# Retention attention with two expert layers: another order of the first twelve attention visits' matmuls, and first weights converted in fixed visits

## The chip, the cores and the metric

One core of a Trainium2 chip runs the kernel. The metric is the device time of one execution in microseconds. Six queues work side by side on a core: TensorE (PE) multiplies, VectorE (DVE), ScalarE (ACT) and GpSimd (POOL) do elementwise work, SyncE (SP) issues most of the DMAs, and each engine works through its own instructions in the order in which they were written, waiting for the others by semaphores.

## The reference

```python
def _attn_ref(q, k, v):                       # (4, 8, 576, 64) each
    scores = scale * np.matmul(q, k.transpose(0, 1, 3, 2))
    gamma = 1.0 - 2.0 ** (-5.0 - np.arange(H))
    Dmat = np.where(rel >= 0, gamma[:, None, None] ** rel[None, :, :], 0.0)
    return np.matmul(scores * Dmat, v)

def _moe_ref(x, w1, w2, w3, w_out):           # x: (2304, 512), d_ff 768
    h = np.maximum(np.maximum(x @ w1, x @ w2), x @ w3)
    return h @ w_out

def _moe2_ref(x, w_gate, w_val, w_out):       # d_ff 1536
    g = x @ w_gate
    return (g * (1.0 / (1.0 + np.exp(-g))) * (x @ w_val)) @ w_out
```

The attention's output, heads side by side, is the first layer's x, and that layer's output is the second's.

## The kernel before

Attention is done in **units**: one of four batches, a pair of heads and one half (288 positions) of the sequence, 32 units in all, in the order batch, pair, half. A half is three chunks of 96 positions. For a unit PE makes: the transposes of k (`tp`, line 249) and those of q with its decay (line 252), both in `a_prep`; the scores of each chunk (`s`, `a_score`, line 272); the chunk's sums of weighted k times v (`m_ps`, `a_state`, line 288), from which ACT and DVE build the running state `st`; and in `a_value` (line 311) the output `o_ps`, which has **v products** (masked scores `pT` times v) and **state products** (`st` times q, six matmuls in a second half and four in a first). The weighted k, `ks`, is a POOL instruction (line 242) at the head of `a_prep`. DVE multiplies the scores by the mask (`pT`, line 274); ACT and DVE split the output into a high and a low part, `xh` and `xl`. A matmul uses the PE array in a shape, rows by columns: transposes of k 96\*128, those of q, v products and m_ps 96\*64, state products 64\*64, scores 64\*96, the dense layers 128\*128. From unit 12 on, the transposes are made by DVE instead.

The first layer's weights come as 64-bit floats. `conv_steps` turns one 128 x 512 piece (a **weight** below, 18 in all) into a high half `wh` and a low half `wlo`, in six phases: two ACT copies `wz` and `wl`, two DVE steps on `wz` (lines 130, 131), one DVE step `wl` (line 133), ACT `wh` (line 141) and POOL `wlo` (line 143). A **slice** (`f_slice`, line 440) is 12 matmuls of one weight with the `xh` and `xl` of one batch half; its result is copied by ACT for the first of three matrices and joined to `hmax` by DVE for the others (line 446). Slices use two rotating PSUM banks (`ps_mm`), a visit's `o_ps` one bank of its own.

The order is written out by hand: a loop of 16 **visits**, one unit each, and then pairs of units. `visit(n)` makes unit n's output, then scores and states of unit n + 1, and in between the preparation of unit n + 2 (`a_prep`), slices and conversion phases. Visits 0 to 7 have no slices; visits 8 to 15 have 4, 4, 4, 4, 4, 4, 6 and 6. `sharing` makes a list of phases from the number of conversions of the visit and spreads it over the gaps between its slices (`share(j)`, ahead of slice j or behind the last one).

Of the kernel before, what the change touches and what calls it, by code (L numbers as in the profile page):

```python
# [10 lines left out]
F32 = mybir.dt.float32  # L11
# [12 lines left out]
P = 128  # L24
NP = H // 2
CK = 96
NC = 3
C = CK * NC
# [41 lines left out]
def retention_moe(ctx, tc, consts, q, k, v, w1, w2, w3, w_out, w_gate, w_val, w_out2, out):  # L70
    nc = tc.nc
    pe, act, dve, pool, sp = nc.tensor, nc.scalar, nc.vector, nc.gpsimd, nc.sync
# [77 lines left out]
    PT = 12  # L150
    PP = 16
# [110 lines left out]
    def a_score(n):  # L262
        if n >= NU:
            return
        b, h, pr = units[n]
        u = U[n]
        s = psa.tile([CK, 2, 512], F32, name="s", tag="s")
        for c in range(NC):
            cs = slice(c * CK, (c + 1) * CK)
            for e in range(2):  # L270
                hd = slice(64 * e, 64 * e + 64)
                pe.matmul(s[:, e, cs], u["kt"][hd, cs], u["qg"][hd, c], start=True, stop=True)  # L272
        pT = att.tile([CK, 2, NC, CK], F32, name="pT", tag="pT")
        dve.tensor_tensor(pT, s[:, :, 0:C].rearrange("p e (c m) -> p e c m", c=NC),
                          d_t[pr].unsqueeze(2).to_broadcast([CK, 2, NC, CK]), ALU.mult)
        u["pT"] = pT

    def a_state(n):

        if n >= NU:  # L280
            return
        b, h, pr = units[n]
        u = U[n]
        nk = NC - h
        m = psa.tile([P, NC, D], F32, name="m_ps", tag="m_ps")
        for c in range(nk):
            for e in range(2):
                pe.matmul(m[64 * e:64 * e + 64, c], u["ks"][:, c, e], u["v"][:, c, e], start=True, stop=True)  # L288
        if h == 0:
            st = states[(b, pr)] = att.tile([P, 2 * NC, D], F32, name="st", tag="st", bufs=2)  # L290
        else:
            st = states.pop((b, pr))
        for c in range(nk):
            g = h * NC + c
            if g == 0:
                act.activation(st[:, 1], m[:, c], ACTF.Copy)
            else:
                dve.scalar_tensor_tensor(st[:, g + 1], st[:, g], e_t[:, pr:pr + 1], m[:, c], ALU.mult, ALU.add)
        u["st"] = st

    def a_value(n):
        b, h, pr = units[n]
        u = U.pop(n)
        o = psa.tile([P, C], F32, name="o_ps", tag="o_ps")
        inter = [(c, e, u["st"][64 * e:64 * e + 64, h * NC + c], u["qg"][64 * e:64 * e + 64, c])
                 for c in range(1 - h, NC) for e in range(2)]
        intra = [(c, e, u["v"][:, c, e], u["pT"][:, e, c]) for c in range(NC) for e in range(2)]
        seen = set()
        parts = intra + inter if n <= NQ0 else inter + intra
        for i, (c, e, l, r) in enumerate(parts):  # L310
            pe.matmul(o[64 * e:64 * e + 64, c * CK:(c + 1) * CK], l, r, start=e not in seen,  # L311
                      stop=(c, e) not in [x[:2] for x in parts[i + 1:]], skip_group_check=True)
            seen.add(e)
        xh, xl = [ffn.tile([P, C], F32R, name=f"x{x}", tag=f"x{x}{pr}", bufs=4) for x in "hl"]
        act.activation(xh, o, ACTF.Copy)
        xs[(2 * b + h, pr)] = (xh, xl)
        return lambda: dve.tensor_tensor(xl, o, f(xh), ALU.subtract)
# [93 lines left out]
    def conv_plan(convs):  # L411

        for _ in range(convs):
            i = wc[0]
            if i < len(win_units):
                wc[0] += 1
                yield (i, 2), (i + 1, 0)
                yield (i, 3), (i + 1, 1)
                yield (i, 4), (i, 5)
# [41 lines left out]
            ps = ps_mm.tile([P, 512], F32, name="psz", tag="mm")  # L461
            pe.matmul(ps.rearrange("p (a m) -> p a m", m=P), zero, zero.unsqueeze(1).to_broadcast([P, 4, P]), start=True, stop=True)

    def sharing(spread, convs, joins):
        plan = list(conv_plan(convs))
        done = 0

        def share(j):
            nonlocal done
            upto = len(plan) * (j + 1) // (spread + 1)  # L470
            for step in plan[done:upto]:
                for i, ph in step:
                    win_phase(i, ph)
            done = upto
            if joins:
                for _ in range(1 if j % 2 else 2):
                    next(early, None)

        return share

    def visit(n, slices, convs):
        share = sharing(slices, convs, False)
        low = a_value(n)
        if slices:
            share(0)
        if n % 2:
            a_load(n // 2 + 3)
        if n % 2 == 0:
            t_load(n // 2 + 2)
        elif n == PP - 1:  # L490
            t_load(PP // 2 + 2)
        if n % (2 * NP) == 2 * NP - 1:
            fq.extend((n // NP - 1 + h, *w) for w in win_units for h in range(2))
        if n < NQ0:
            a_score(n + 1)
            low()
            a_state(n + 1)
            late = []
        elif n + 1 < PP:
            a_state(n + 1)  # L500
            low()
            a_score(n + 1)
            late = []
        else:
            low()
            swap_banks()
            late = pair_next(PP // 2)
        ahead = [n + 2] if n < PP - 2 else [PP, PP + 1] if n < PP - 1 else [PP + 2, PP + 3]
        for j in range(slices + 1):
            if late:  # L510
                late.pop(0)()
            if j == min(2, slices - 1) or not slices:
                a_prep(ahead.pop(0))
            if j == 4 and ahead:
                a_prep(ahead.pop(0))
            if j or not slices:
                share(j)
            if j < slices:
                f_some(1)
# [82 lines left out]
    def tables(pr):  # L602
        g = 2 * NC
        (pool if pr else dve).tensor_tensor(
            dia[pr].rearrange("p a e m -> p (a e) m"), ident.unsqueeze(1).to_broadcast([CK, g, CK]),
            q_t[:, g * pr:g * pr + g].unsqueeze(2).to_broadcast([CK, g, CK]), ALU.mult)
        pool.tensor_tensor(d_t[pr], mask.unsqueeze(1).to_broadcast([CK, 2, CK]),
                           s_t[:, 2 * pr:2 * pr + 2].unsqueeze(2).to_broadcast([CK, 2, CK]), ALU.mult)
# [7 lines left out]
    a_prep(0)  # L616
    spin(2)
    a_score(0)
    a_prep(1)
    a_state(0)  # L620
    for n in range(PP):
        if n < NP - 1:
            tables(n + 1)
        if 2 <= n < 6:
            win_load(n - 2)
        if n == 5:
            win_phase(0, 0)
            win_phase(0, 1)
        if n == 9:
            sp.dma_start(out=cst_g, in_=consts[:, O_G:NCONST])  # L630
        visit(n, *((0, 0) if n < 5 else (0, 1) if n < 8 else (4, 2) if n < 13 else (4, 3) if n < 14 else (6, 2)))
        if n == 15:
            ask(1)
    for j in range(PP // 2, NU // 2):
# [442 lines left out]
```

## Time and profile before

| | us |
|---|---|
| runs | 818.52, 820.24, 821.1 |
| median of the three | 820.24 |
| the profiled execution | 818.73 |
| its span, first to last instruction | 816.9 |
| PE busy in it | 808.5 (99%) |
| DVE busy | 563.2 (69%) |
| ACT busy | 315.1 (39%) |
| POOL busy | 211.1 (26%) |

The granted TensorE clock is at its full level in all of the span's forty slices. A row of the order of time gives the start and the length of an instruction or of a run of like ones, and in brackets how long the engine had been idle and what ended that. Matmuls overlap, so the length of a piece is best read from one row's start to the next row's start.

### The profile page before, as it was taken

To read this page: it belongs to the slowest core of one execution; us is meant where nothing else is said; L and a number is where in the kernel's file an instruction comes from. 1 tells how busy PE (TensorE), PEld (TensorE's weight loads), DVE (VectorE), ACT (ScalarE), POOL (GpSimd) and SP (SyncE) were. 2 spreads that over 40 slices of the span, in tenths; PEclk is the share of its full clock that TensorE was granted. 3 is DMA by queue.
4 is the path that set the end of the run, shared out by engine and by line. 5 is a ranking of instruction groups with operands and counts; after the bars stand their busy time and mean duration, and the time that the engine had idled before them with its cause. 6 is when DMAs were issued, how large, how long until landed. Compare 5 with 4: busy or idle time off the path is not lost.

```text
span 816.9 us, 15439 instructions
## 1 busy us (share of the span) xinstructions
PE 808.5 (99%) x5924; PEld 759.6 (93%) x5924; DVE 563.2 (69%) x1008; ACT 315.1 (39%) x633; POOL 211.1 (26%) x193
## 2 busy tenths in 40 slices
PE   9999999999999999999999999999999999999998
PEld 6799899999999999999999999999999999999996
DVE  3768857777774245586387889998888865455555
ACT  3654514324322133664345534444444322332220
POOL 5344320000000003342032223332332233322331
PEclk9999999999999999999999999999999999999999
DMA  9999779999963143964534343444322016666522
GB/s 193 243 227 206 167 148 238 260 249 240 252 184 113 64 137 106 285 159 149 190 116 157 127 149 141 149 168 153 132 77 71 20 65 243 208 232 219 200 97 77
DMA packets 158201, 135.08 MB, mean 165 GB/s; under 512 B 94000, under 2 KB 132912, under 8 KB 158128
## 3 DMA queue, kind: packets, MB, share of 16 engines
q1 hardware_dynamic: 157568, 133.69, 57.4%
q8 instruction: 46, 0.75, 0.4%
q10 hardware_dynamic: 560, 0.42, 0.2%
q14 instruction: 27, 0.22, 0.1%
HBM read 89.77 MB, written 44.30 MB: 164 GB/s over the span
## 4 chain that ended last, share of the span: by engine, by line
PE 93%; DVE 4%; ACT 1%; issue 1%; DMA 0%; POOL 0%; SPq 0%; ACTq 0%; DVEq 0%
PE g L945 31%; PE ps L440 28%; PE ps L922 18%; PE ps L869 7%; PE o_ps L311 2%; PE s L272 1%; PE o_ps L332 1%; PE s L362 1%; PE o_ps L327 1%; PE tp L252 1%; PE m_ps L288 1%; PE s L355 0%; DMA kn<-in_k_dram 0%; PE tp L249 0%; DVE acc L927 0%
## 5 line engine op out<-in xcount | busy, mean ns | idle before, releaser
L440 PE MATMUL ps<-xl,wh 128*128 128x288 f32 x576 | 172.2, 299 | 1.8 <-DVE hmax L446 1.2
L440 PE MATMUL ps<-xh,wh 128*128 128x288 f32 x576 | 169.8, 295 | 0.0
L440 PE MATMUL ps<-xh,wlo 128*128 128x288 f32 x576 | 169.6, 294 | 0.0
L993 POOL TENSOR_TENSOR gl<-p,gh 128x384 fp32r<-128x384 f32 x72 | 86.0, 1212 | 287.3 <-ACT gh L992 277.5
L922 PE MATMUL ps<-wp,gh 128*128 128x512 f32 (+1 forms) x436 | 135.6, 392 | 0.4 <-DVE acc L927 0.3
L440 PEld LDWEIGHTS ps<-xl,wh 128*128 128x128 f32 x576 | 108.0, 188 | 5.2 <-DVE hmax L446 2.4
L440 PEld LDWEIGHTS ps<-xh,wlo 128*128 128x128 f32 x576 | 108.1, 188 | 0.0
L440 PEld LDWEIGHTS ps<-xh,wh 128*128 128x128 f32 x576 | 108.1, 188 | 0.0
L922 PEld LDWEIGHTS ps<-wp,gh 128*128 128x128 f32 x436 | 80.5, 188 | 15.0 <-DVE acc L927 1.5
L922 PE MATMUL ps<-wp,gl 128*128 128x512 f32 (+1 forms) x218 | 85.6, 393 | 0.0
L446 DVE TENSOR_TENSOR hmax<-ps,hmax 128x288 f32<-128x288 f32 x96 | 43.5, 454 | 58.1 <-PE ps L440 49.1
L927 DVE TENSOR_TENSOR acc<-ps,acc 128x512 f32<-128x512 f32 (+1 forms) x91 | 61.8, 682 | 27.8 <-PE ps L922 26.6
L945 PE MATMUL g<-xhB,wa 128*128 128x384 f32 x288 | 73.3, 336 | 0.0
L945 PE MATMUL g<-xhT,wc 128*128 128x384 f32 x288 | 73.2, 335 | 0.0
L672 POOL TENSOR_TENSOR hl<-hf,hh 128x384 fp32r<-128x384 f32 x26 | 30.6, 1186 | 133.7 <-ACT hh L671 131.5
L992 ACT ACTIVATE gh<-p 128x384 fp32r<-128x384 f32 x72 | 37.9, 526 | 58.6 <-DVE p L996 51.6
L981 ACT ACTIVATE sb<-u 128x384 f32<-128x384 f32 x36 | 18.9, 525 | 100.3 <-DVE u L979 99.2
L242 POOL TENSOR_TENSOR ks<-kn,cst_a 96x384 f32<-96x384 f32 (+1 forms) x32 | 24.6, 779 | 115.5 <-PE s L355 105.4
L444 ACT ACTIVATE hmax<-ps 128x288 f32<-128x288 f32 x48 | 19.7, 410 | 84.5 <-PE ps L440 83.3
L945 PEld LDWEIGHTS g<-xhB,wa 128*128 128x128 f32 x288 | 52.1, 188 | 0.0
L945 PEld LDWEIGHTS g<-xhT,wc 128*128 128x128 f32 x288 | 52.0, 188 | 0.0
L973 DVE TENSOR_TENSOR p<-g,p 128x384 f32<-128x384 f32 x36 | 19.9, 554 | 43.8 <-PE g L945 34.7
(134 smaller groups left out, 1699.1 us busy)
## 6 DMA issues: line engine op xcount, KB each, us to landing
w<-in_moe_w_out_dram SPq DMA_DIRECT2D x18, 512.0 KB, 4.1
w<-l_d SPq DMA_DIRECT2D x28, 256.0 KB, 3.0
h_d<-hmax SPq DMA_DIRECT2D x48, 144.0 KB, 3.1
w<-in_moe_w_dram SPq DMA_DIRECT2D x12, 512.0 KB, 7.1
w<-in_moe_w_gate_dram SPq DMA_DIRECT2D x12, 512.0 KB, 5.3
w<-in_moe_w_val_dram SPq DMA_DIRECT2D x12, 512.0 KB, 5.5
vn<-in_v_dram SPq DMA_DIRECT2D x16, 288.0 KB, 7.6
out_dram<-acc SPq DMA_DIRECT2D x17, 256.0 KB, 2.0
```

What stands on the lines that cost most here:

```text
L242: pool.tensor_tensor(u["ks"][:, 0:nk], u["k"][:, 0:nk], sc, ALU.mult)
L440: pe.matmul(ps, l[:, ksl], r, start=n == 0, stop=n == 3 * KD - 1)
L444: act.activation(mx[hb], ps, ACTF.Copy)
L446: dve.tensor_tensor(mx[hb], ps, mx[hb], ALU.max)
L672: (dve if fi in (3, 5) and hx else pool).tensor_tensor(hl, hf, f(hh), ALU.subtract)
L869: pe.matmul(ps[:, 0:HT], l[:, es], rr, start=n == 0, stop=n == 3 * F1 - 1)
L922: pe.matmul(ps[:, cs], l[:, sl], r[:, cs], start=n == 0, stop=n == 3 * GRP - 1)
L927: dve.tensor_tensor(a[:, cs], ps[:, cs], a[:, cs], ALU.add)
L945: pe.matmul(ps, l[:, ks], r[:, kc], start=first and n == 0, stop=n == 5, skip_group_check=True)
L973: dve.tensor_tensor(p5, g2, p5, ALU.add)
L992: act.activation(gh[half], t, ACTF.Copy)
L993: pool.tensor_tensor(gl[half], t, f(gh[half]), ALU.subtract)
```

## The change

Visits 0 to 7 get a function of their own, `visit_first`, and `a_value` takes a hook `between`. A visit now prepares unit n + 1 first (`a_prep(n + 1)`, up to unit 11), then does unit n's v products, the hook (the states of unit n + 1), unit n's state products, and the scores of unit n + 1. Visit 7 does the states behind the scores, as before. In visits 0 to 7 the output is put into the slices' two banks (`o_mm`). The low part `xl` of a visit is made in the next one. Tables `FIRST` and `NEXT` name the phases of the first weights in visits 4 to 8, one weight and a half fewer than before by the end of visit 7; the count of conversions starts again at weight 4 with visit 9. Visits 8 to 15 now have 4, 4, 4, 4, 4, 5, 6 and 5 slices, and conversions of 2, 3, 2, 2, 3 and 2 weights in visits 9 to 14.

```diff
@@ -298,19 +298,23 @@
                 dve.scalar_tensor_tensor(st[:, g + 1], st[:, g], e_t[:, pr:pr + 1], m[:, c], ALU.mult, ALU.add)
         u["st"] = st
 
-    def a_value(n):
+    def a_value(n, between=lambda: None):
         b, h, pr = units[n]
         u = U.pop(n)
-        o = psa.tile([P, C], F32, name="o_ps", tag="o_ps")
-        inter = [(c, e, u["st"][64 * e:64 * e + 64, h * NC + c], u["qg"][64 * e:64 * e + 64, c])
-                 for c in range(1 - h, NC) for e in range(2)]
-        intra = [(c, e, u["v"][:, c, e], u["pT"][:, e, c]) for c in range(NC) for e in range(2)]
-        seen = set()
-        parts = intra + inter if n <= NQ0 else inter + intra
-        for i, (c, e, l, r) in enumerate(parts):
-            pe.matmul(o[64 * e:64 * e + 64, c * CK:(c + 1) * CK], l, r, start=e not in seen,
-                      stop=(c, e) not in [x[:2] for x in parts[i + 1:]], skip_group_check=True)
-            seen.add(e)
+        if n < NQ0:
+            o = ps_mm.tile([P, 512], F32, name="o_mm", tag="mm")[:, 0:C]
+        else:
+            o = psa.tile([P, C], F32, name="o_ps", tag="o_ps")
+        for c in range(NC):
+            for e in range(2):
+                pe.matmul(o[64 * e:64 * e + 64, c * CK:(c + 1) * CK], u["v"][:, c, e], u["pT"][:, e, c],
+                          start=c == 0, stop=c < 1 - h, skip_group_check=True)
+        between()
+        for c in range(1 - h, NC):
+            for e in range(2):
+                hd = slice(64 * e, 64 * e + 64)
+                pe.matmul(o[hd, c * CK:(c + 1) * CK], u["st"][hd, h * NC + c], u["qg"][hd, c],
+                          start=False, stop=True, skip_group_check=True)
         xh, xl = [ffn.tile([P, C], F32R, name=f"x{x}", tag=f"x{x}{pr}", bufs=4) for x in "hl"]
         act.activation(xh, o, ACTF.Copy)
         xs[(2 * b + h, pr)] = (xh, xl)
@@ -461,8 +465,8 @@
             ps = ps_mm.tile([P, 512], F32, name="psz", tag="mm")
             pe.matmul(ps.rearrange("p (a m) -> p a m", m=P), zero, zero.unsqueeze(1).to_broadcast([P, 4, P]), start=True, stop=True)
 
-    def sharing(spread, convs, joins):
-        plan = list(conv_plan(convs))
+    def sharing(spread, convs, joins, plan=None):
+        plan = plan or list(conv_plan(convs))
         done = 0
 
         def share(j):
@@ -478,11 +482,45 @@
 
         return share
 
+    FIRST = {4: ((0, 0), (0, 1)), 5: ((0, 2),), 6: ((0, 3), (1, 0), (0, 4), (0, 5)), 7: ((1, 1), (1, 2))}
+    NEXT = [((1, 3), (2, 0), (1, 4), (1, 5)), ((2, 1),), ((2, 2), (3, 0)), ((2, 3), (3, 1)), ((2, 4), (2, 5)),
+            ((3, 2),), ((3, 3), (4, 0)), ((3, 4), (3, 5), (4, 1))]
+    rest = []
+
+    def visit_first(n):
+
+        if n < NP - 1:
+            tables(n + 1)
+        if n % 2 == 0 and n < 6:
+            win_load(n // 2)
+        elif n in (1, 3):
+            a_load(n // 2 + 3)
+        elif n == 5:
+            win_load(3)
+        if n == 0:
+            a_state(0)
+        a_prep(n + 1)
+        while rest:
+            rest.pop()()
+        for i, ph in FIRST.get(n, ()):
+            win_phase(i, ph)
+        if n >= 6:
+            a_load(n - 1)
+        rest.append(a_value(n, (lambda: a_state(n + 1)) if n < NQ0 - 1 else (lambda: None)))
+        if n == NQ0 - 1:
+            fq.extend((n // NP - 1 + h, *w) for w in win_units for h in range(2))
+        a_score(n + 1)
+        if n == NQ0 - 1:
+            a_state(n + 1)
+            rest.pop()()
+            wc[0] = 4
+
     def visit(n, slices, convs):
-        share = sharing(slices, convs, False)
-        low = a_value(n)
-        if slices:
-            share(0)
+        share = sharing(slices, convs, False, NEXT if n == NQ0 else None)
+        if n + 1 < PT:
+            a_prep(n + 1)
+        low = a_value(n, (lambda: a_state(n + 1)) if n + 1 < PP else (lambda: None))
+        share(0)
         if n % 2:
             a_load(n // 2 + 3)
         if n % 2 == 0:
@@ -491,29 +529,22 @@
             t_load(PP // 2 + 2)
         if n % (2 * NP) == 2 * NP - 1:
             fq.extend((n // NP - 1 + h, *w) for w in win_units for h in range(2))
-        if n < NQ0:
-            a_score(n + 1)
-            low()
-            a_state(n + 1)
-            late = []
-        elif n + 1 < PP:
-            a_state(n + 1)
-            low()
+        low()
+        if n + 1 < PP:
             a_score(n + 1)
             late = []
         else:
-            low()
             swap_banks()
             late = pair_next(PP // 2)
         ahead = [n + 2] if n < PP - 2 else [PP, PP + 1] if n < PP - 1 else [PP + 2, PP + 3]
         for j in range(slices + 1):
             if late:
                 late.pop(0)()
-            if j == min(2, slices - 1) or not slices:
+            if j == 2 and ahead[0] >= PT:
                 a_prep(ahead.pop(0))
-            if j == 4 and ahead:
+            if j == 4 and ahead and ahead[0] >= PT:
                 a_prep(ahead.pop(0))
-            if j or not slices:
+            if j:
                 share(j)
             if j < slices:
                 f_some(1)
@@ -616,19 +647,12 @@
     a_prep(0)
     spin(2)
     a_score(0)
-    a_prep(1)
-    a_state(0)
-    for n in range(PP):
-        if n < NP - 1:
-            tables(n + 1)
-        if 2 <= n < 6:
-            win_load(n - 2)
-        if n == 5:
-            win_phase(0, 0)
-            win_phase(0, 1)
+    for n in range(NQ0):
+        visit_first(n)
+    for n in range(NQ0, PP):
         if n == 9:
             sp.dma_start(out=cst_g, in_=consts[:, O_G:NCONST])
-        visit(n, *((0, 0) if n < 5 else (0, 1) if n < 8 else (4, 2) if n < 13 else (4, 3) if n < 14 else (6, 2)))
+        visit(n, *((4, 2) if n < 10 else (4, 3) if n < 11 else (4, 2) if n < 13 else (5, 3) if n < 14 else (6, 2) if n < 15 else (5, 2)))
         if n == 15:
             ask(1)
     for j in range(PP // 2, NU // 2):
```

Three places, in the order in which the instructions stand on an engine. **PE, visit 1**: transposes of unit 2 (kn, qn), then unit 1's output (pT and vn are the v products, kq and st the state products), scores of unit 2 (s) and its states (m_ps); a row with x6 stands for six matmuls. Before:

```order
L249 MATMUL tp<-cst_a,kn 128x96 x3
L252 MATMUL tp<-dia_83,qn 64x96 x6
L311 MATMUL o_ps<-pT,vn 64x96 x6
L311 MATMUL o_ps<-kq,st 64x96 x6
L272 MATMUL s<-kq 96x96 x6
L288 MATMUL m_ps<-vn,ks 64x64 x6
```

Now:

```order
L249 MATMUL tp<-cst_a,kn 128x96 x3
L252 MATMUL tp<-dia_83,qn 64x96 x6
L310 MATMUL o_mm<-pT,vn 64x96 x6
L288 MATMUL m_ps<-vn,ks 64x64 x6
L316 MATMUL o_mm<-kq,st 64x96 x6
L272 MATMUL s<-kq 96x96 x6
```

The states (m_ps) have moved from the end of the visit to a place between v products and state products.

**POOL, around visits 8 and 9.** ks is the weighted k of a unit: ks_660, ks_768 and ks_907 are units 9, 10 and 11 before; the wlo are the low halves of weights 1 to 5. Before:

```order
L143 TENSOR_TENSOR wlo_551<-wl_557,wh_550 128x512
L242 TENSOR_TENSOR ks_660<-kn_393,cst_a_80 96x256
L143 TENSOR_TENSOR wlo_609<-wl_615,wh_608 128x512
L242 TENSOR_TENSOR ks_768<-kn_506,cst_a_80 96x384
L143 TENSOR_TENSOR wlo_677<-wl_683,wh_676 128x512
L143 TENSOR_TENSOR wlo_704<-wl_751,wh_703 128x512
L242 TENSOR_TENSOR ks_907<-kn_506,cst_a_80 96x256
```

Now, with ks_649, ks_799 and ks_940 for units 9, 10 and 11, and the same weights:

```order
L242 TENSOR_TENSOR ks_649<-kn_362,cst_a_80 96x256
L143 TENSOR_TENSOR wlo_547<-wl_604,wh_546 128x512
L143 TENSOR_TENSOR wlo_688<-wl_727,wh_687 128x512
L143 TENSOR_TENSOR wlo_732<-wl_753,wh_731 128x512
L242 TENSOR_TENSOR ks_799<-kn_552,cst_a_80 96x384
L143 TENSOR_TENSOR wlo_791<-wl_796,wh_790 128x512
L143 TENSOR_TENSOR wlo_843<-wl_877,wh_842 128x512
L242 TENSOR_TENSOR ks_940<-kn_552,cst_a_80 96x256
```

The ks of unit 10 stood ahead of the low half of weight 3 and now stands behind it; the ks of unit 11 stood ahead of weight 5's and now stands behind it.

**DVE, the end of visit 8 and what follows** in the changed kernel: hmax_725 and hmax_748 take the visit's third and fourth slice, wz_733 and wl_753 are steps of weight 3, st_827 is the state of unit 10.

```order
L450 TENSOR_TENSOR hmax_725<-ps_755,hmax_725 128x288
L130 TENSOR_SCALAR wz_733<-wz_733 128x512
L131 SCALAR_TENSOR_TENSOR wz_733<-w64e_473,wz_733 128x512
L450 TENSOR_TENSOR hmax_748<-ps_773,hmax_748 128x288
L133 ISA wl_753<-wz_733,wl_753 128x1024
L298 SCALAR_TENSOR_TENSOR st_827<-st_827,cst_a_80,m_ps_820 128x64 x2
```

The step wl of weight 3, on which its high and low halves hang, stands behind the hmax of the visit's last slice.

## Rows read from the trace of the kernel before

**Rows 1.** Part 4 of the page: the chain that ended last, by engine.

```profile
PE 93%; DVE 4%; ACT 1%; issue 1%; DMA 0%; POOL 0%; SPq 0%; ACTq 0%; DVEq 0%
```

**Rows 2.** PE's waits in the whole span: total us, times, longest us.

```profile
PE ps L440 <- DVE hmax L446: 1.2, 1, 1.2
PE o_ps L311 <- DVE xl L317: 1.2, 2, 0.7
```

**Rows 3.** Windows: length, busy time per engine, granted clock, DMA share, GB/s; visits 14 and 15.

```profile
92.00:106.00 14.00, 12.78 (x126) 11.87 (x126) 13.29 (x26) 5.16 (x10) 6.30 (x5) 1.00 0.34 69
```

**Rows 4.** PE in order of time, visits 0 to 10: start us, us, instruction.

```profile
7.27 0.47 PE L249 MATMUL tp<-cst_a,kn 96*128 96x96 f32 x3
...
10.94 0.47 PE L249 MATMUL tp<-cst_a,kn 96*128 96x96 f32 x3
...
11.94 0.72 PE L311 MATMUL o_ps<-pT,vn 96*64 96x96 f32 x12
12.59 0.71 PE L311 MATMUL o_ps<-kq,st 64*64 64x96 f32 x12
...
13.91 0.57 PE L288 MATMUL m_ps<-vn,ks 96*64 96x64 f32 x12
14.41 0.47 PE L249 MATMUL tp<-cst_a,kn 96*128 96x96 f32 x3
...
30.77 0.47 PE L249 MATMUL tp<-cst_a,kn 96*128 96x96 f32 x3
...
38.93 0.40 PE L440 MATMUL ps<-xl,wh 128*128 128x288 f32 x1
...
47.22 0.72 PE L311 MATMUL o_ps<-pT,vn 96*64 96x96 f32 x12
47.76 0.52 PE L288 MATMUL m_ps<-vn,ks 96*64 96x64 f32 x12
48.21 0.75 PE L272 MATMUL s<-kq 64*96 64x96 f32 x12
...
56.53 0.55 PE L311 MATMUL o_ps<-kq,st 64*64 64x96 f32 x8
```

**Rows 5.** SP's queue in order of time: the issue of v's first load.

```profile
2.69 0.47 SPq L191 DMA_DIRECT2D vn<-in_v_dram  x1
```

**Rows 6.** DMA issues between 2.6 and 3.2 us: count, KB each, us to landing.

```profile
vn<-in_v_dram SPq DMA_DIRECT2D x1, 288.0 KB, 5.1
```

**Rows 7.** The chain in order of time, slices of visits 8 and 11.

```profile
39.00 3.38 PE ps L440 x24
...
67.52 6.56 PE ps L440 x48
```

**Rows 8.** DVE in order of time, around the end of visit 8.

```profile
46.79 0.45 DVE L446 TENSOR_TENSOR hmax<-ps,hmax 128x288 f32<-128x288 f32 x1
47.16 0.68 DVE L133 CUSTOM_DVE_ANT_0 wl<-wz,wl 128x1024 uint16<-128x1024 uint16 x1
47.76 0.42 DVE L130 TENSOR_SCALAR wz<-wz 128x512 uint32<-128x512 uint32 x1
48.21 0.69 DVE L131 SCALAR_TENSOR_TENSOR wz<-w,wz 128x512 uint32<-128x512 uint32 x1
```

**Rows 9.** ACT in order of time, visits 8 and 9.

```profile
47.87 0.63 ACT L141 ACTIVATE wh<-wl 128x512 fp32r<-128x512 f32 x1 [1.30 <-DVE wl L133]
...
56.64 0.41 ACT L444 ACTIVATE hmax<-ps 128x288 f32<-128x288 f32 x1 [0.63 <-PE ps L440]
...
57.52 0.61 ACT L141 ACTIVATE wh<-wl 128x512 fp32r<-128x512 f32 x1
```

**Rows 10.** POOL in order of time, visits 9 and 10.

```profile
50.01 0.61 POOL L242 TENSOR_TENSOR ks<-kn,cst_a 96x256 f32<-96x256 f32 x1
...
58.22 1.29 POOL L143 TENSOR_TENSOR wlo<-wl,wh 128x512 fp32r<-128x512 f32 x1 [2.35 <-ACT wh L141]
59.47 0.82 POOL L242 TENSOR_TENSOR ks<-kn,cst_a 96x384 f32<-96x384 f32 x1
```

## Prediction

> **What bounds the kernel now.** The chain that ended last comes first. It says that 93% of the span is TensorE (PE) executing, 4% VectorE (DVE) and 1% ScalarE (ACT) [rows 1]. So an edit is worth what it does to PE's own order and to PE's waits. The list of PE's waits then shows how little waiting there is in the part that changes: 1.2 us for DVE's xl, in two waits of at most 0.7, and one wait of 1.2 us for a DVE hmax [rows 2]. The second lies between 92 and 106 us, a stretch in which PE is busy 12.78 of 14 us at a granted clock of 1.00, which is the 2.4 GHz level [rows 3]. Third, PE's order of time for the first sixteen visits gives the length of each piece, from one start to the next [rows 4]. In visit 1 the v products take 0.65 us (11.94 to 12.59) where the state products, of another shape (64\*64 instead of 96\*64), follow them. In visit 9 they take 0.54 (47.22 to 47.76) where m_ps, of the same shape, follows. m_ps takes 0.50 between two other shapes (13.91 to 14.41) and 0.45 behind v products (47.76 to 48.21). The reader is to see a fixed price for a change of shape, 0.05 to 0.11 us, which no column of the matmuls themselves explains.
>
> **The change, part by part.** The sum is made against the profiled execution: 818.73 us, of which the span is 816.9. The median of the three runs, 820.24, is 1.51 above it; that difference is added at the end. E is the moment at which a visit's last slice ends and PE goes on.
>
> *Visit 0.* m_ps of unit 0 moves from behind the second q transposes to directly behind s, where PE arrives at 7.27 [rows 4]. It needs v's first load: issued at 2.69 [rows 5], landing 5.1 us later [rows 6], at 7.79. PE waits 7.79 - 7.27 = 0.52 us where the transposes covered it before. One change of shape less gives 0.16 back (next step): **+0.36**. The ks of unit 1 now stands behind a dia and a dm on POOL; PE asks for it only behind v, some 2 us later, and I cost that at nothing. If the DMA lands late, each tenth costs a tenth.
>
> *Visits 1 to 6.* The m_ps of the next unit moves between the v products and the state products: 0.65 becomes 0.54 and 0.50 becomes 0.45, so 0.16 less per visit: 6 x 0.16 = **-0.96**. Six visits take 30.77 - 10.94 = 19.83 us now, 3.305 each [rows 4]. What could eat it: m_ps stood ahead of the next transposes and gave DVE time for pT. Now only transposes, 1.00 us (10.94 to 11.94), lie between s and the v products that read pT. In visit 9, whose pT has slices to cover it, this never shows, so the cost here is bounded by 0 and by one m_ps, 0.50 a visit. I take 0: DVE has only pT to do at that moment.
>
> *Visits 7 and 8.* From 30.77 to the first slice at 38.93 PE spends 8.16 us for two visits that take 2 x 3.305 = 6.61 undisturbed. The 1.55 more contain the two waits of 1.2 for xl [rows 2]: two accumulators of visits now rotate through the slices' banks instead of one, and conversions are thinned to less than one weight per visit, so DVE reaches xl in time. If that cover failed, 1.55 would stay. Visit 8 saves its 0.16 too: -1.55 - 0.16 = **-1.71**.
>
> *Visits 9 and 10.* The four slices of a visit were two stretches of two, 3.38 us each with the transposes between (the second reads the same within 0.01), and become one stretch of four, 6.56 as in visit 11 [rows 7]: 2 x 3.38 - 6.56 = 0.20 per visit, for visits 8 and 9: **-0.40**.
>
> *The wait that is added.* Before, ks of unit n + 2 was issued on POOL in the middle of visit n's slices. Now ks(n + 1) is issued at the start of visit n, behind everything that the last share of visit n - 1 has put on POOL. For visit 9 that is the low half (wlo) of weight 3. Its chain starts only at E, since DVE does the hmax of visit 8's last slice ahead of the step wl. From rows: the slice's reader starts 0.11 after E (56.53 [rows 4] to 56.64 [rows 9]); hmax to wl 0.37 and wl to wh 0.71 (46.79, 47.16 [rows 8], 47.87 [rows 9]); wh to wlo 0.70 (57.52 [rows 9], 58.22 [rows 10]); wlo to ks 1.25, ks itself 0.82 [rows 10]. ks(10) is there at E + 3.96. PE needs it after transposes (1.00) and v products (0.54), at E + 1.54. It waits 3.96 - 1.54 = **+2.42**. Behind m_ps on PE stand the state products, the scores and the next four slices, so nothing fills the gap; DVE stands at the state update, ACT at st. In visit 10 the same happens to ks(11), behind the low half of weight 5: copy of the last slice to wh 0.88 (56.64 to 57.52 [rows 9]), so 0.11 + 0.88 + 0.70 + 1.25 and ks of two chunks 0.61 (50.01 [rows 10]) = 3.55, less 1.54: **+2.01**. From visit 11 on, units are prepared early again and the wait ends. Bounds of both together: nothing, if POOL were ahead, and 5.1, if DVE and ACT reach the slice's result 0.3 later each time.
>
> A rule that bears on this term: in the trace no PE wait in these visits is over 1.2 us, and around it the granted clock stays at 1.00 [rows 2, 3]; by the rows the waits cost their length and no more. The Trainium skill, page "TensorE: Matmul & The Clock Gate", section "Why this matters for your kernels", asks for no idle gaps between bursts of matmuls, as a gap brings the lower clock back; no run shown here has a gap of 2 us. What that would cost is a rival below.
>
> *Visits 13 to 15.* The slices per visit change from 4, 6, 6 to 5, 6, 5 with the same three conversions in visit 13. A slice is 6.56 / 4 = 1.64 us [rows 7], more than the 1.2 us by which DVE was late with an hmax in visit 14 [rows 2]; DVE gets that slice's time one visit earlier: **-1.2**. Bounds: 0 and -1.2. In visit 15 the state products now stand between v products and the pair's states: one change of shape more, **+0.16**.
>
> *Loads.* The first weight's load now stands on SP's queue ahead of the fourth k, q and v, and the fifth weight's ahead of the sixth: each delays those by one 512 KB transfer. They are wanted in visits 5 and 9; in the trace PE waits for no load there, and I cost them at nothing and leave a late landing to the range.
>
> **Sum:** 0.36 - 0.96 - 1.71 - 0.40 + 2.42 + 2.01 - 1.2 + 0.16 = +0.68. 818.73 + 0.68 = 819.4, and with 1.51 for the median **820.9 us**. The gains (4.27) and the new waits (4.43) about cancel. A difference under 0.3%, 2.5 us, can't be told from none.
>
> **Rivals.**
> 1. *ks is in time.* If the last conversion step of visits 8 and 9 is done inside the slices, PE does not wait and the sum is 0.68 - 4.43 = -3.75: 816.5. For it: POOL is lightly used there, and one kind of wait is read from queue order alone. Against: the order puts wl behind the last slice's hmax in the one case and wh behind its copy in the other, and both end at E or later. Chance 0.17.
> 2. *Slower: DVE becomes late in visit 10.* That visit now carries three conversions in four slices, as visit 13 does before. One conversion is wz 0.45, 0.69 and wl 0.60 on DVE [rows 8], 1.74, three are 5.2, and four hmax at 0.37 are 1.5, besides the visit's own DVE work, within four slices of 6.56 and an attention part of 3.3. It starts late, as DVE stood still in the wait. If an hmax comes later than the slice two behind it, PE pays what visit 14 pays now, 1.2, and the same backlog carried on keeps visit 14's 1.2 too: 0.68 + 2.4 = +3.1: 823.3. Against: unlike visit 14 there are no conversions left over from a visit before. Chance 0.15.
> 3. *The waits bring the lower clock.* At half clock, the four slices behind a wait take up to 6.56 us more: 827.5 for one. Against: no lowered stretch in this trace. Chance 0.05.
> 4. *The change does not do what it says:* shapes side by side save nothing, because the 0.16 belongs to visit 9's neighbours. Then 0.96 + 0.16 + 0.40 come back: 822.5. Against: it shows in both pieces of one row sequence. Chance 0.06.
>
> **How the numbers follow.** The forecast has 0.57. Its own terms, with visit 14's wait kept and the bounds of the added waits, spread from 819 to 823. The range 816.8 to 824.4 takes in rivals 2 and 4 and part of rival 1; outside lie half of 1, all of 3 and the edge of 2, about 0.16. Faster by over 0.3%: nearly all of rival 1 and a little of the forecast, 0.19. Slower: rival 2, rival 3 and the upper part of the forecast, 0.27. Within 0.3%: 0.54.
>
> **What the profile of the changed kernel would show.** Right: the first slice starts near 36.6 us instead of 38.93; no PE wait for xl; two PE waits at m_ps for ks on POOL, 2.4 and 2.0 us, in visits 9 and 10; no wait for hmax near 100 us; granted clock 1.00. Wrong: no PE wait for POOL (rival 1), a wait for hmax in visit 11 (rival 2), a stretch below 1.00 behind a wait (rival 3), v products of 0.65 with m_ps behind them (rival 4), or PE waiting for a k, q or v load in visits 5 to 9.

## The result, and the profile after

| | us |
|---|---|
| the changed kernel, median of 5 runs (831.12 to 832.8) | 831.6 |
| the kernel before beside it, median of 5 (818.52 to 821.1) | 819.43 |
| ratio, with its 95% interval | 1.0147 [1.0132, 1.0162] |
| profiled execution, and its span | 832.8, 831.0 |

The change makes the kernel slower by 12.2 us. The forecast was 820.9, within a range of 816.8 to 824.4.

The chain that ended last (part 4 of the page) answers to [rows 1]: PE's share of it went from 93% to 84%.

```profile
PE 84%; DVE 7%; issue 3%; DMA 3%; ACT 2%; POOL 1%; DVEq 0%; SPq 0%; ACTq 0%; POOLq 0%
```

PE's waits in the whole span (total us, times, longest) answer to [rows 2]. No wait for xl is left; two for ks and five for DVE's hmax took its place, two of the five before 130 us.

```profile
PE ps L444 <- DVE hmax L450: 5.9, 5, 2.3
PE m_ps L288 <- POOL ks L242: 5.5, 2, 3.4
PE ps L444 <- ACT hmax L448: 1.0, 2, 0.5
```

PE in order of time answers to [rows 4]: start, length, instruction, and in brackets the idle time before it.

```profile
36.03 0.40 PE L444 MATMUL ps<-xl,wh 128*128 128x288 f32 x1
...
43.38 0.67 PE L310 MATMUL o_ps<-pT,vn 96*64 96x96 f32 x12
47.42 0.91 PE L288 MATMUL m_ps<-vn,ks 96*64 96x64 f32 x12 [3.37 <-POOL ks L242]
48.26 1.23 PE L316 MATMUL o_ps<-kq,st 64*64 64x96 f32 x12
49.41 1.28 PE L272 MATMUL s<-kq 64*96 64x96 f32 x12
...
61.86 0.45 PE L288 MATMUL m_ps<-vn,ks 96*64 96x64 f32 x8 [2.11 <-POOL ks L242]
...
77.75 0.40 PE L444 MATMUL ps<-xl,wh 128*128 128x288 f32 x1 [0.53 <-ACT hmax L448]
83.21 0.75 PE L272 MATMUL s<-kq 64*96 64x96 f32 x12 [0.66 <-DVE kq L259]
89.59 0.37 PE L444 MATMUL ps<-xl,wh 128*128 128x288 f32 x1 [2.26 <-DVE hmax L450]
...
104.79 0.37 PE L444 MATMUL ps<-xl,wh 128*128 128x288 f32 x1 [1.38 <-DVE hmax L450]
```

The first slice starts at 36.03 instead of 38.93: up to there the change has gained 2.90 us. Then comes the first wait for ks, and what follows it is slow: m_ps takes 0.91 us against 0.52, the scores 1.28 against 0.75 [rows 4]. The windows (length, busy time of PE, PEld, DVE, ACT, POOL, granted clock, DMA share, GB/s) answer to [rows 3] and say why:

```profile
45.00:50.00 5.00, 2.58 (x31) 2.24 (x32) 1.30 (x4) 2.02 (x6) 2.05 (x2) 0.63 0.97 257
50.00:55.00 5.00, 5.00 (x34) 4.83 (x31) 2.47 (x5) 1.28 (x3) 0.00 (x0) 0.69 1.26 245
...
60.00:65.00 5.00, 3.14 (x34) 2.84 (x35) 2.57 (x6) 1.98 (x4) 1.81 (x2) 0.83 1.06 171
65.00:70.00 5.00, 5.00 (x33) 5.00 (x33) 2.68 (x7) 1.38 (x3) 1.50 (x2) 0.83 0.45 144
...
80.00:85.00 5.00, 4.34 (x58) 3.86 (x57) 4.93 (x10) 1.88 (x3) 1.27 (x1) 1.00 1.22 269
85.00:90.00 5.00, 2.74 (x21) 2.54 (x20) 4.93 (x10) 2.17 (x4) 2.53 (x2) 1.00 0.66 147
90.00:95.00 5.00, 5.00 (x35) 4.83 (x35) 4.07 (x8) 2.06 (x5) 1.28 (x1) 0.66 0.77 218
```

Around and behind each of the three longest waits the mean granted clock of a window is below 1.00: PE was at the 1.2 GHz level for part of that window. In the kernel before every slice of the page was at full clock. From 80 us on another thing shows: DVE is busy 4.93 of 5 us, and PE waits for it.

The pairs of units begin at 129.68 us instead of 117.78. So 11.90 + 2.90 = 14.8 us were lost between 36 and 130 us. The account by rows: 5.48 in the two waits for ks; 4.83 in the four later waits (two for DVE's hmax, one for its kq, one for ACT's hmax), where the kernel before waits 1.19; and the rest, about 5.7, mostly at the lower clock (the run with PE kept busy, below, gives 5.1). Behind 130 us this execution has 2.2 us more in three waits for an hmax, at 178, 240 and 245 us. They differ from run to run (0.7 there in *ks early*, none in the mid-slice kernel, both below), and the medians differ by 12.2, so little of the loss lies there.

### The profile page after: what moved, and what is told of

Same layout as the page of the kernel before. It is cut to its first block, busy times and chain, and to the rows that moved or that the text cites. A ratio compares the mean times of both kernels' runs of the same rounds, so it can differ in the third digit from the quotient of the medians.

```text
span 831.0 us, 15434 instructions
## 1 busy us (share of the span) xinstructions
PE 812.7 (98%) x5924; PEld 764.7 (92%) x5924; DVE 571.2 (69%) x1008; ACT 315.3 (38%) x633; POOL 210.5 (25%) x193
## 4 chain that ended last, share of the span: by engine, by line
PE 84%; DVE 7%; issue 3%; DMA 3%; ACT 2%; POOL 1%; DVEq 0%; SPq 0%; ACTq 0%; POOLq 0%
PE g L969 31%; PE ps L444 21%; PE ps L946 17%; PE ps L893 7%; PE s L272 1%; DVE wz L131 1%; PE o_ps L336 1%; DVE wz L130 1%; PE tp L252 1%; DMA l_d<-w64e 1%; PE s L366 1%; DMA w<-in_moe_w_out_dram 1%; PE o_ps L331 1%; POOL wlo L143 1%; DMA w<-in_moe_w_val_dram 1%
## 5 line engine op out<-in xcount | busy, mean ns | idle before, releaser
L444 PE MATMUL ps<-xl,wh 128*128 128x288 f32 x576 | 174.0, 302 | 6.9 <-DVE hmax L450 5.9
L444 PE MATMUL ps<-xh,wh 128*128 128x288 f32 x576 | 171.6, 298 | 0.0
L444 PEld LDWEIGHTS ps<-xl,wh 128*128 128x128 f32 x576 | 109.9, 191 | 10.4 <-issue 4.2
L444 PEld LDWEIGHTS ps<-xh,wlo 128*128 128x128 f32 x576 | 109.9, 191 | 0.0
L444 PEld LDWEIGHTS ps<-xh,wh 128*128 128x128 f32 x576 | 109.8, 191 | 0.0
```

What stands on the lines that cost most here:

```text
L444: pe.matmul(ps, l[:, ksl], r, start=n == 0, stop=n == 3 * KD - 1)
```

## The experiments

All times are medians; the ratio is against the kernel before on the same chip, with its 95% interval. "Mid-slice" is the kernel of the section "Units prepared in the middle of the slices".

| run | us | ratio |
|---|---|---|
| changed kernel | 831.6 | 1.0147 [1.0132, 1.0162] |
| ks early | 823.81 | 1.0050 [1.0035, 1.0065] |
| third conversion later | 827.87 | 1.0106 [1.0091, 1.0121] |
| ks early and conversion later | 820.5 | 1.0020 [1.0010, 1.0029] |
| mid-slice kernel | 819.75 | 1.0015 [1.0003, 1.0027] |
| PE busy in the waits | 826.5 | 1.0073 [1.0048, 1.0097] |
| mid-slice, three early conversions | 834.08 | 1.0155 [1.0111, 1.0199] |
| mid-slice, early conversions spread | 821.53 | 1.0031 [1.0003, 1.0058] |
| mid-slice, low halves left out | 815.56 | 0.9934 [0.9908, 0.9960] |
| kernel before, state first | 822.37 | 1.0039 [1.0024, 1.0054] |
| mid-slice, state after | 816.65 | 0.9968 [0.9955, 0.9980] |
| the same again | 817.05 | 0.9971 [0.9946, 0.9997] |
| mid-slice, preparation sooner | 820.65 | 1.0029 [1.0012, 1.0046] |
| mid-slice, both orders | 817.15 | 0.9966 [0.9949, 0.9984] |
| changed kernel, state after | 827.39 | 1.0092 [1.0059, 1.0124] |
| ks early, state after | 819.65 | 0.9992 [0.9969, 1.0014] |

### ks early, the third conversion later, and both

*ks early* splits `a_prep`: bind and ks in `a_ks`, the transposes where they were.

```diff
+            if j == 2 and n in (8, 9):
+                a_ks(n + 2)
```

> Theory Q (queue order): the two waits for ks on POOL (3.4 and 2.1 us) start the loss, and each brings the lower clock behind it (m_ps, state products, scores and four slices longer by about 2.5 and 2.0 us); 10 us together. With ks of units 10 and 11 issued in the middle of the slices before, both go: 831.6 - 10 = 821.6, and if the later waits for hmax in visits 11 to 13 (4.8 us) are a consequence of DVE standing still in those waits, they go too: about 817. Rival L (conversion layout): the backlog of the three conversions in visit 10 is there by itself: 821.6, with waits of 2 us for hmax on DVE near 80 us still in the trace. Rival S (the new order of shapes costs in itself): hardly better than 828.

*The third conversion* of visit 10 goes to visit 14:

```diff
-        visit(n, *((4, 2) if n < 10 else (4, 3) if n < 11 else (4, 2) if n < 13 else (5, 3) if n < 14 else (6, 2) if n < 15 else (5, 2)))
+        visit(n, *((4, 2) if n < 13 else (5, 3) if n < 14 else (6, 3) if n < 15 else (5, 2)))
```

> The third conversion of visit 10 goes to visit 14, the ks waits stay. Theory Q with the backlog as a consequence of the waits: 829 to 831.6, the waits for ks of 3.4 and 2.1 us unchanged. Rival L: the waits for hmax and kq of visits 11 to 13 and the clock that they cost (4.8 us) go: about 826.8.

> Both edits, ks of units 10 and 11 early and the third conversion in visit 14. Q and L alike: 816 to 818, about 2 to 3 us below the kernel before, granted clock 1.00 throughout the attention. If it stays above 820, a third cause is at work.

Measured: 823.81 (-7.8), 827.87 (-3.7) and 820.5 (-11.1). Both edits gain, and the two gains add up almost exactly. But the first is smaller than the 10 of its account, and with both undone the kernel is still 0.2% slower than before, not 2 to 3 us faster. PE's waits with ks early:

```profile
PE ps L450 <- DVE hmax L456: 4.2, 4, 2.2
PE s L278 <- ACT kq L260: 1.6, 2, 1.4
PE ps L450 <- ACT hmax L454: 1.3, 2, 0.8
```

The waits for ks are gone. New ones have come: the copy of the transposes (kq on ACT) is late at the start of a visit, and DVE is as late with hmax as before. A third cause was at work.

### Units prepared in the middle of the slices: the mid-slice kernel

From visit 8 on, ks and transposes are where the kernel before has them; visits 0 to 7 and the order of shapes are those of the change; the third conversion is in visit 14.

```diff
-        if n + 1 < PT:
+        if n == NQ0:
             a_prep(n + 1)
...
-            if j == 2 and ahead[0] >= PT:
+            if j == 2:
                 a_prep(ahead.pop(0))
```

> From visit 8 on, units are prepared whole (ks, transposes) in the middle of the slices as in the kernel before, with visits 0 to 7 as in the changed kernel and the third conversion in visit 14. The first part brought the first slice 2.9 us earlier; if all the loss lies behind it, this is 819.4 - 2.9 = 816.5, within 1 us of the kernel with both edits. Rival: late conversions (weights half a conversion further behind at visit 8) cost 1 to 2 us by themselves: 818.

Measured: 819.75, 3 us above what was expected. In its trace the lead over the kernel before holds until visit 12, whose v products start at 71.39 where the kernel before starts that visit at 74.00. It goes in two waits for hmax, in visits 12 and 13 (an expectation below calls them 11 and 12):

```profile
78.12 0.37 PE L444 MATMUL ps<-xl,wh 128*128 128x288 f32 x1 [1.25 <-DVE hmax L450]
...
92.20 0.37 PE L444 MATMUL ps<-xl,wh 128*128 128x288 f32 x1 [1.39 <-DVE hmax L450]
```

### Was it the clock? PE kept busy in the waits

The changed kernel, with matmuls on zeros ahead of the late m_ps:

```diff
+        def between():
+            if n in (9, 10):
+                ps = ps_mm.tile([P, 512], F32, name="psz", tag="mm")
+                for _ in range(14 if n == 9 else 8):
+                    pe.matmul(ps.rearrange("p (a m) -> p a m", m=P), zero, zero.unsqueeze(1).to_broadcast([P, 4, P]), start=True, stop=True)
+            a_state(n + 1)
...
```

> The changed kernel with 14 and 8 matmuls on zeros put on PE between the v products and the late state products of visits 9 and 10 (about 3.0 and 1.7 us of work at the upper clock, within the waits of 3.4 and 2.1). The waits for ks stay, but PE works in them. If idling brings the lower clock: granted clock 1.00 from 40 to 75 us, slices of visits 9 and 10 back at 6.56 us, 831.6 - 4.5 = 827.1. If the lower clock comes from something else: 831.6 and the same stretches below 1.00.

Measured: 826.5, so 5.1 us less, although ks comes no earlier. PE in order of time, and a window behind the first wait:

```profile
44.37 3.20 PE L526 MATMUL psz<-zero 128*128 128x512 bf16 x14
47.82 0.57 PE L288 MATMUL m_ps<-vn,ks 96*64 96x64 f32 x12 [0.25 <-POOL ks L242]
48.32 0.71 PE L316 MATMUL o_ps<-kq,st 64*64 64x96 f32 x12
...
86.07 0.37 PE L444 MATMUL ps<-xl,wh 128*128 128x288 f32 x1 [2.24 <-DVE hmax L450]
```

```profile
50.00:55.00 5.00, 5.00 (x40) 5.00 (x39) 4.28 (x8) 1.54 (x4) 1.30 (x1) 1.00 1.19 285
```

m_ps starts at 47.82 instead of 47.42, in both 4.9 us behind the last slice of visit 8, but it takes 0.57, and the clock stays at 1.00. Filling the two waits took all three low stretches away, the one near 90 us too, although the wait ahead of that one stayed (2.24 instead of 2.26). So PE's idling has a part in the lower clock, and the clock costs about 5 us here beside the 5.5 of waiting; why the third stretch went with the others is not shown.

### What makes DVE late: too few weights ahead, or POOL?

Two edits of the mid-slice kernel convert more before visit 8, one with three whole weights in visits 5 to 7 as in the kernel before, one with one step per visit from visit 4 on:

```diff
-    FIRST = {4: ((0, 0), (0, 1)), 5: ((0, 2),), 6: ((0, 3), (1, 0), (0, 4), (0, 5)), 7: ((1, 1), (1, 2))}
+    FIRST = {5: ((0, 0), (0, 1))}
...
+        if n >= 5:
+            sharing(0, 1, False)(0)
```

> The kernel with units prepared in the middle of the slices kept its 2.6 us lead up to visit 11 and lost it in visits 11 and 12, where DVE is busy 18.9 of 20 us and PE waits 1.25 and 1.39 us for an hmax. Here the first three weights are converted whole in visits 5, 6 and 7, as in the kernel before; the rest as in that run. Theory D (DVE, one conversion behind, is the bound from 60 to 95 us): these two waits go, -2.6, and DVE's overrun in visits 5 to 7 gives back 0 to 1.5: 817 to 818.7. Rival P (POOL's low halves and DVE's steps happen to fall on each other, whatever was converted before): about 819.7 again, waits moved elsewhere.

```diff
+    FIRST = {3: ((0, 0), (0, 1)), 4: ((0, 2),), 5: ((0, 3), (0, 4), (0, 5)), 6: ((1, 0), (1, 1), (1, 2)), 7: ((1, 3), (2, 0), (1, 4), (1, 5), (2, 1))}
```

> As that run, but two weights and the first step of a third are converted by the end of visit 7, one step of DVE per visit from visit 4 on, in DVE's idle time there. Theory D: half a conversion less behind, so one of the two waits goes or both shrink, and no overrun in visits 5 to 7: 817.5 to 818.5. Rival P: 819.7.

A third one lets POOL write zeros in place of the subtraction:

```diff
-        sub_eng.tensor_tensor(lo, box[0], f(hi), ALU.subtract)
+        if sub_eng is pool:
+            pool.memset(f(lo), 0.0)
```

> The kernel with units prepared in the middle of the slices; the low halves of the first eighteen weights are set to zero by POOL instead of being computed from two tiles (that part of the computation is left out). If POOL's subtraction is what lengthens DVE's steps beside it, L131's mean goes from 1.03 back to 0.69 us, kq's from 1.07 to 0.55, DVE's busy time to 120 us falls by about 8 us, and the waits of 1.25 and 1.39 for an hmax go: 816.5 to 817.3. If it is only that DVE has one conversion more to do behind visit 8 (D without the port), the steps keep their length and it stays at 819.7.

Measured: 834.08, 821.53 and 815.56. More weights ahead do not help: with half a weight more the waits of 1.25 and 1.39 us stand unchanged. With three whole weights PE's list has this row:

```profile
PE m_ps L288 <- POOL ks L242: 8.3, 3, 4.2
```

It is the change's own fault over again, now in visits 6 to 8: ks at a visit's start stands on POOL behind the wlo of the visit before. So the thinner conversions in the first visits are what the order "ks at the start" needs. Behind them PE still waits 1.25 and 1.44 us for an hmax in that trace. Theory D (DVE's backlog of conversions is the bound) falls. Without POOL's subtraction the waits go and the time is the lowest of all, for part of the work. DVE's groups up to 120 us (count, total, mean ns), first of the mid-slice kernel, then with the low halves left out:

```profile
L131 DVE SCALAR_TENSOR_TENSOR wz<-w,wz 128x512 uint32<-128x512 uint32 x12 | 12.4, 1029 | 0.4
...
L259 DVE TENSOR_TENSOR kq<-qt,cst_g 128x288 f32<-128x288 f32 x8 | 8.5, 1066 | 0.3
```

```profile
L131 DVE SCALAR_TENSOR_TENSOR wz<-w,wz 128x512 uint32<-128x512 uint32 x12 | 8.3, 692 | 0.4
...
L262 DVE TENSOR_TENSOR kq<-qt,cst_g 128x288 f32<-128x288 f32 x8 | 3.7, 458 | 0.3
```

These two read two tiles in SBUF each, as wlo does on POOL, and they lose all their excess; so does wl (L133), which reads two tiles as well, from 778 to 684 ns. L130, which reads one, keeps its mean (612 and 600). In the kernel before L131 and kq take 800 and 548. The same DVE steps are dearer in the mid-slice kernel, since more of them fall on a wlo. Which edit brought that?

### The order on DVE

In the kernel before, visits from 8 on issue a conversion step (`share(0)`) ahead of the state update st. In the change the states stand in the hook, so st comes first. That edit alone, put into the kernel before (PE's order stays; ACT's copy for a unit's first state, L296, moves along):

```diff
         low = a_value(n)
+        if NQ0 <= n < PP - 1:
+            a_state(n + 1)
         if slices:
             share(0)
...
         elif n + 1 < PP:
-            a_state(n + 1)
             low()
```

> The kernel before with one thing of the change alone: in visits 8 to 14 the state update (st, two steps of 0.3 us on DVE) is issued ahead of the first conversion step of the visit instead of behind it; PE's order stays. Theory O: the second step of that conversion (L131) then starts 0.5 us later, just behind the start of POOL's wlo instead of just ahead of it, and takes 1.7 us instead of 0.7; DVE falls behind and PE gets waits of 1.25 and 1.39 us for an hmax: 819.4 + 2.6 = 822. Rival (DVE's work behind visit 8 decides, not its order): 819.4, L131's mean stays at 0.80.

And taken back in the mid-slice kernel: `a_state` makes the matmuls in the hook and returns the update of st, which is called behind `share(0)`.

```diff
-        low = a_value(n, (lambda: a_state(n + 1)) if n + 1 < PP else (lambda: None))
+        chains = []
+        low = a_value(n, (lambda: chains.append(a_state(n + 1, True))) if n + 1 < PP else (lambda: None))
...
+        for c in chains:
+            c()
         low()
```

> The kernel with units prepared in the middle of the slices, with the state update back behind the first conversion step; PE's order as in the changed kernel. Theory O: L131's mean back near 0.8 us, no waits of 1.25 and 1.39 for an hmax in visits 11 and 12: 819.7 - 2.6 = 817.1, below the kernel before. Rival: 819.7.

Measured: 822.37 and 816.65, as forecast to 0.5 us: +2.9 in the one, -3.1 in the other. Up to 120 us L131's mean goes from 800 to 952 ns in the one and from 1029 to 816 in the other, kq's from 548 to 924 and from 1066 to 640 (the other's second profile). The mechanism in visit 12: DVE and then POOL in the kernel before,

```profile
75.14 0.42 DVE L130 TENSOR_SCALAR wz<-wz 128x512 uint32<-128x512 uint32 x1
75.59 0.69 DVE L131 SCALAR_TENSOR_TENSOR wz<-w,wz 128x512 uint32<-128x512 uint32 x1
76.20 0.59 DVE L298 SCALAR_TENSOR_TENSOR st<-st,cst_a,m_ps 128x64 f32<-128x64 f32 x2
```

```profile
75.97 1.48 POOL L143 TENSOR_TENSOR wlo<-wl,wh 128x512 fp32r<-128x512 f32 x1 [2.74 <-ACT wh L141]
```

and with the state first:

```profile
77.33 0.59 DVE L298 SCALAR_TENSOR_TENSOR st<-st,cst_a,m_ps 128x64 f32<-128x64 f32 x2
77.83 0.42 DVE L130 TENSOR_SCALAR wz<-wz 128x512 uint32<-128x512 uint32 x1
78.29 1.71 DVE L131 SCALAR_TENSOR_TENSOR wz<-w,wz 128x512 uint32<-128x512 uint32 x1
```

```profile
78.15 1.30 POOL L143 TENSOR_TENSOR wlo<-wl,wh 128x512 fp32r<-128x512 f32 x1 [3.45 <-ACT wh L141]
```

In the first L131 starts 0.38 us ahead of wlo and takes 0.69, and wlo is stretched (1.48 against 1.30). In the second it starts 0.14 us behind wlo and takes 1.71. Whoever comes first goes through; the other waits. A fixed distance decides: wlo follows DVE's wl by some 1.4 us (wl, ACT's wh, the signals), and st puts 0.5 us between wl and L131. The Trainium skill, page "SBUF — State Buffer", section "Who interferes with whom", states this as a rule: a DVE instruction with two inputs in SBUF and a GpSimd instruction that reads SBUF block each other for a whole instruction, and the issue order decides who is blocked; a GpSimd instruction that only writes does not block such a one. Both halves agree with the rows here (1.71 beside wlo; 692 and 458 ns beside the memset).

Two more runs on the same matter: the next unit prepared one slice sooner (`j == 1` for `j == 2` up to visit 13), so that kq is made ahead of the visit's first wlo, alone and with the state after.

> The same kernel with the preparation of the next unit one slice sooner (before the second slice instead of the third), so that DVE's kq product is done before the visit's first wlo starts instead of beside it. If kq's 1.07 us (0.46 where no low half is computed) is part of the lateness: mean of kq near 0.5, waits for an hmax smaller by some 1 us: 818.5. Rival: other steps fall on wlo instead: 819.7 or above.

> Both orders on DVE. If both are right, the least collision of all: 816 to 817; what is left of the waits for hmax under 1 us in total.

Measured: 820.65 and 817.15. kq does get shorter, but wl (L133), which reads two tiles as well, now falls on wlo: its mean is 910 ns against 778 (without the state after). Moving one step out of the way moved another in; nothing is gained.

### Is the third conversion a cause of its own?

The order restored in the changed kernel, alone and with ks early:

> The changed kernel with only the state update of visits 8 to 14 put back behind the visit's first conversion step on DVE. The waits for ks and the lower clock behind them stay (10 us). Theory O (the order on DVE makes steps fall on wlo): the waits for hmax, kq and the clock behind the one of 2.3 us shrink: 827 to 828.5. If the third conversion in visit 10 makes these waits by itself: 831.6.

> ks of units 10 and 11 early and the state update behind the conversion step; the three conversions stay in visit 10. With ks early alone it was 823.8. If the third conversion costs 3.3 us by itself, order gives only its 3.1: 820.7. If that cost too is steps of DVE that fall on wlo: 817 to 818.

Measured: 827.39 (-4.2) and 819.65. The first is as the order theory has it: the wait of 2.26 shrinks to 0.90. The second lies between the two forecasts. With the conversion in visit 14 and the units prepared mid-slice it is 817.05, so some 2.6 us belong to the third conversion and to the kq copy together; by how much each was not separated.

### The version that beats both

Mid-slice kernel with the state after, once more:

> The fastest kernel so far once more, without any edit, for its interval and for a profile without the late v load at the start: 816.65 before; 816 to 817.5 expected, faster than the kernel before by 0.25 to 0.4%.

Measured: 817.05, ratio 0.9971 [0.9946, 0.9997], after 0.9968 [0.9955, 0.9980]: 2.3 to 2.9 us faster than the kernel before. PE's waits in its span of 814.4 us:

```profile
PE ps L450 <- DVE hmax L456: 1.1, 2, 0.9
...
PE m_ps L288 <- DMA vn<-in_v_dram: 0.7, 1, 0.7
```

## Why the prediction was wrong

**Visits 0 to 8 (right but for visit 0).** Terms of +0.36, -0.96 and -1.71 make -2.3; the first slice came 2.90 earlier: -0.07, -1.00 and -1.83. Shapes side by side save, pT was never late, no xl wait is left. The term of visit 0 was the one that missed, and it varies: v's load made no wait in the changed kernel's profile and one of 0.65 us in that of the best version.

**Visits 9 and 10, the waits (right in kind, mis-sized).** Forecast 2.42 and 2.01, measured 3.37 and 2.11. The missing 0.95 is a DVE step ahead of the chain, which the rows used did not show: DVE and POOL around the end of visit 8's slices at 42.49,

```profile
41.47 1.42 DVE L130 TENSOR_SCALAR wz<-wz 128x512 uint32<-128x512 uint32 x1
42.92 0.69 DVE L131 SCALAR_TENSOR_TENSOR wz<-w64e,wz 128x512 uint32<-128x512 uint32 x1
43.53 0.45 DVE L450 TENSOR_TENSOR hmax<-ps,hmax 128x288 f32<-128x288 f32 x1
43.90 0.68 DVE L133 CUSTOM_DVE_ANT_0 wl<-wz,wl 128x1024 uint16<-128x1024 uint16 x1
```

```profile
41.31 1.28 POOL L143 TENSOR_TENSOR wlo<-wl,wh 128x512 fp32r<-128x512 f32 x1 [2.99 <-ACT wh L141]
45.31 1.27 POOL L143 TENSOR_TENSOR wlo<-wl,wh 128x512 fp32r<-128x512 f32 x1 [2.72 <-ACT wh L141]
46.54 0.82 POOL L242 TENSOR_TENSOR ks<-kn,cst_a 96x384 f32<-96x384 f32 x1
```

L130 takes 1.42 us instead of 0.42 [rows 8] beside a wlo, so the hmax that was to start 0.11 behind the slice starts 1.04 behind it. From there every step is as forecast: 0.37, 0.71, 0.70 (to POOL's 45.31), 1.23.

**"The waits cost their length and no more" (the step that failed).** It was argued from waits of at most 1.2 us [rows 2, 3] to waits of 2.0 and 2.4, which came as 2.11 and 3.37. The lower clock, a term at nothing in the sum, came with them and with a wait of 2.26 for an hmax, and cost about 5 us, as much as the waits for ks. Rival 3 named it, with a chance of 0.05, and priced one stretch at 6.56; there were three, partial ones. The rule that the prediction weighed against the rows, in the Trainium skill's page "TensorE: Matmul & The Clock Gate", section "Why this matters for your kernels", was the better guide: the rows had nothing to say on waits of that length.

**Visits 13 to 15 (wrong sign).** The -1.2 for the gone hmax wait did not come. PE waited for DVE from visit 12 on (kq at 83.21, hmax at 89.59 and 104.79), 4.30 us in all, and 0.53 for ACT's hmax in visit 11. Rival 2, which put DVE's lateness into visit 10 and priced it at 2.4, was right in kind and too low.

**What was not in the sum.** The move of st ahead of a conversion step on DVE. The prediction followed PE's order and POOL's queue and gave DVE's own order no term; the edit alone costs 2.9 us in the kernel before and 4.2 in the changed kernel.

Up to 130 us the trace came out at +11.90 against the forecast's +0.68. Of the 11.2 between them the first visits make -0.6, the two waits for ks 1.05, the later waits 4.8 (3.64 more than before, where -1.2 was forecast), and about 5.9 is left, which is the clock in the main.

The sum as the runs give it: the first visits -2.3 to -2.9; ks at the visit's start, with the clock, about +8; the third conversion +3.3 to 3.7; the state first about +3. That is roughly 819.4 + 12 = 831.4. The prices overlap: the third conversion's was taken with the state first, and with the state after what is left for it and the kq copy together is 2.6.

## What to carry to other kernels

Where a change puts an instruction of a lightly used engine at a later place, price the wait twice: by its length, and, if TensorE idles for longer than any wait in the trace, by the lower clock on what follows; a few cheap matmuls in the gap tell the two apart. When edits move work between DVE and GpSimd, look not at the sums but at which of two instructions that read SBUF starts first: a shift of half a microsecond, made by a cheap instruction, took a step from 0.69 to 1.71 us, and PE waited for an engine that is idle 31% of the span. Undo edits one by one; here the change was one good part (2.9 us) beside three bad ones.

## What the runs showed of the hardware that was not expected

The clock fell behind waits of 3.37, 2.11 and 2.26 us, but in the run with PE busy in the waits it stayed at 1.00 behind one of 2.24. The length of a wait alone does not tell. In one execution of the best version (821.92 us, the profile of its first run) PE waited for the load of v half a microsecond longer than in the second profile, and this row of PE and this window follow; in the second profile the same stretch has a clock of 1.00.

```profile
8.76 0.57 PE L288 MATMUL m_ps<-vn,ks 96*64 96x64 f32 x12 [1.13 <-DMA vn<-in_v_dram]
```

```profile
9.00:20.00 11.00, 11.00 (x131) 9.54 (x126) 2.80 (x8) 2.57 (x6) 4.16 (x6) 0.53 1.25 206
```

So 0.5 us more waiting went with 5.7 us more span (820.1 against 814.4), where the prediction has "each tenth costs a tenth" for visit 0. That the wait is the cause is not shown. In the profile of *ks early* a wait of 0.97 us at the same place is followed by a clock of 1.00. And in that of *mid-slice, preparation sooner* (an execution of 825.63 us) PE does not wait for v and the granted clock reads 1.00 in every window there, but from 5.2 to 20.4 us its matmuls take as long as they do at the 1.2 GHz level, the scores 1.28 us instead of 0.75:

```profile
7.34 1.28 PE L272 MATMUL s<-kq 64*96 64x96 f32 x12
```

If PE was at the lower level there, the granted clock does not show it; only the lengths of the matmuls do.

L130, which reads one tile, was held up even beside a POOL instruction that only writes: with the low halves left out, DVE and then POOL read

```profile
72.95 1.28 DVE L130 TENSOR_SCALAR wz<-wz 128x512 uint32<-128x512 uint32 x1
```

```profile
72.41 0.61 POOL L245 TENSOR_TENSOR ks<-kn,cst_a 96x256 f32<-96x256 f32 x1 [6.28 <-PE m_ps L291]
72.96 0.98 POOL L144 MEMSET wlo<- 128x512 f32 x2
```

Undisturbed it takes 0.42 [rows 8]; ks covers only the first 0.07 us of it, the two memsets the rest.
